# Mamba-2 scan with a gated feed-forward: g in four 32-row products over four PSUM banks, states from 32-column products, two hp banks with a lag of two, running products in halves, another order of the start

**Chip, cores, metric.** One NeuronCore of a Trainium2 chip. Time is device microseconds of one execution. A profile is one execution; its span is mostly 1.7 to 2 us shorter than the time of the same execution.

## The reference, cut to what matters

```python
# attention part: x (4, 8, 768, 32), a (4, 8, 768), B and C (4, 8, 768, 16)
for c in range(nc):                                   # chunks
    L = np.exp(cum[:, :, :, None] - cum[:, :, None, :]) * causal
    y_intra = np.einsum('bhij,bhjd->bhid', (Cc @ Bc^T) * L, xc)
    y_inter = np.einsum('bhin,bhnd->bhid', Cc, state) * np.exp(cum)
    state = decay_full * state + sum_j(Bc x xc * decay_from_j)
# feed-forward part on the rows of y: 3072 tokens, 256 -> 2048 -> 256
h = x @ w_in
g = h * np.cos(h)
out = g @ w_out
```

The kernel works in blocks of 128 steps (six blocks c) with four sequences b of eight heads. The feed-forward part is cut into 96 tiles n of 128 hidden rows by 512 tokens (16 per block). All products are float32. The scan of block c+1 runs beside the feed-forward of block c. "A period" below is three tiles n with one sequence b of the scan among them: its transposes in the first, its `g` in the second, its `y` and states in the third.

## The kernel before

The parts that the change and the argument touch (cuts are marked `# ...`):

```python
BANKS = {"scan": 3, "h": 3, "o": 2}                   # PSUM banks: 8
LAG = 3

def decays(c, b):                                      # running products of a
    # ... c > 0:
    V.tensor_tensor_scan(out=l, data0=arow.pop((c, b)), data1=unit, initial=0.0,
                         op0=ALU.mult, op1=ALU.add)    # 128 x 1024
    V.tensor_tensor_scan(out=r, data0=along[c][:, b], data1=ones, ...)   # reach

def turn(c, b):
    tp = bank([P, 2, P], "tp")
    PE.transpose(tp[:, 0], B...); PE.transpose(tp[:, 1], C...)
    for t in range(HH):                                # 4
        ACT.activation(cT[:, t], tp[:, 1], AF.Copy, scale=slot[:, t:t + 1])
    ACT.copy(out=bcT[:, 0], in_=tp[:, 0])
    V.tensor_tensor(out=bcT[:, 1], in0=tp[:, 1], in1=reach[c, b], op=ALU.mult)

def intra(c, b):
    g = [bank([P, HH, P], "g") for _ in range(2)]
    for u in range(2):
        r = slice(64 * u, 64 * u + 64)
        PE.matmul(g[u], lhsT=bcT[r, 0], rhs=cT[r], start=True, stop=True)
    # ... VectorE: m = g * l

def carry(c, b):
    s_ps = bank([P, H, D], "s_ps")
    PE.matmul(s_ps, lhsT=sc, rhs=xr[:, b], start=True, stop=True)  # 128 x 256
    # ... VectorE: state = s_ps * own + state * reach

for n in range(NC * NF + LAG):
    first(n)       # hp = w_in^T yT; ScalarE: k; VectorE: w
    grade(...)     # ScalarE, GpSimd: conversion of the weights, n < 13
    gate(n - 1)    # ScalarE: Sin; VectorE: gT = hp * cos
    second(n - LAG)   # o += gT^T w_out; at the end of a block, copies of o
    join(...)      # VectorE, GpSimd: conversion of the weights
    # ... carry(0, n); for the next block: decays, then turn, intra or finish
```

## Time and profile before

| | before |
|---|---|
| time, median (range) | 432.41 us (431.49 to 433.74) |
| span of the profile | 430.6 us |
| TensorE busy | 97% |
| hp(0) starts | 27.40 us |
| hp(0) to hp(18), weights converted beside it | 77.2 us |
| a period after that | 13.46 us |

The main lines are in the prediction. For the stages I take the start of the first matmul of hp(n) for each n; a difference between two kernels that changes between hp(i) and hp(j) was won or lost there. The group lines of the two parts that the change aims at, with count, busy time and mean duration in ns:

```profile
L298 PE MATMUL g<-cT,bcT 64*128 64x512 f32 x96 | 27.8, 641 | 0.3 <-ACT bcT L286 0.2
L333 PE MATMUL s_ps<-xr,sc 128*128 128x256 f32 x40 | 13.6, 421 | 0.0
```

Each float32 product shows as two matmul instructions. Their recorded durations contain latency and overlap, so the sums of busy time are no measure of what a product costs the stream; start-to-start distances are.

### The profile page before, as it was taken

How to read it: one execution, taken by the hardware profiler on the slowest of the kernel's cores; microseconds unless marked ns; L12 is line 12 of the kernel's file. 1: busy time of each engine (PE TensorE's matmuls, PEld its weight loads, DVE VectorE, ACT ScalarE, POOL GpSimd, SP SyncE). 2: the span in 40 equal slices, each digit the busy share in tenths (PEclk: the TensorE clock that was granted, in tenths of full speed). 3: DMA queues.
4: the chain of work that ended last, by engine and by line, in shares of the span. 5: the costliest groups of instructions: out<-in, count | busy, mean ns of one | idle time of the engine just before them, and what ended most of it. 6: DMA issues, size and time to landing. Idle time of an engine off the chain costs nothing.

```text
span 430.6 us, 5067 instructions
## 1 busy us (share of the span) xinstructions
PE 419.0 (97%) x1886; PEld 270.4 (63%) x1886; DVE 263.6 (61%) x388; ACT 178.3 (41%) x376; POOL 46.2 (11%) x62
## 2 busy tenths in 40 slices
PE   8988989989999999999999999999999999999996
PEld 8645555656566666666657656566665666666665
DVE  4868998984765574656764467665476555443332
ACT  2457565623443343533433434342343433333332
POOL 2155365340000000000000000000000000000000
PEclk9999999999999999999999999999999999999999
DMA  8999994185301157111129111102010000010001
GB/s 95 329 117 331 318 144 103 34 116 57 98 7 45 49 98 74 52 47 49 50 66 105 50 49 49 50 0 75 0 49 2 0 2 0 2 50 0 0 2 49
DMA packets 105945, 30.25 MB, mean 70 GB/s; under 512 B 75136, under 2 KB 101824, under 8 KB 105920
## 3 DMA queue, kind: packets, MB, share of 16 engines
q1 hardware_dynamic: 105920, 29.92, 34.3%
q8 instruction: 15, 0.25, 0.2%
q14 instruction: 10, 0.08, 0.1%
HBM read 26.57 MB, written 3.34 MB: 69 GB/s over the span
## 4 chain that ended last, share of the span: by engine, by line
PE 81%; DVE 6%; SPq 5%; DMA 2%; ACT 2%; issue 2%; POOL 1%; ACTq 0%; DVEq 0%
PE hp L349 35%; PE o L370 34%; SPq L109 4%; PE g L298 4%; PE y L319 3%; PE s_ps L333 2%; PE y L315 2%; POOL w_in L187 1%; DVE mag L183 1%; DVE lam L250 1%; DMA words<-in_moe_w_out_dram 1%; DVE mag L181 1%; SPq L126 1%; DMA along<-a_all 1%; DVE gT L362 1%
## 5 line engine op out<-in xcount | busy, mean ns | idle before, releaser
L349 PE MATMUL hp<-yT,w_in 128*128 128x512 f32 x384 | 183.3, 600 | 5.2 <-POOL w_in L187 3.2
L370 PEld LDWEIGHTS o<-w_out,gT 128*128 128x128 f32 x768 | 146.0, 190 | 59.4 <-issue 44.5
L370 PE MATMUL o<-w_out,gT 128*128 128x256 f32 x768 | 181.0, 379 | 0.0
L355 DVE SCALAR_TENSOR_TENSOR w<-hp,k 128x512 f32<-128x512 f32 x96 | 66.1, 688 | 120.0 <-ACT k L353 120.0
L353 ACT ACTIVATE k<-hp 128x512 int32<-128x512 f32 x96 | 57.3, 597 | 186.6 <-PE hp L349 186.2
L349 PEld LDWEIGHTS hp<-yT,w_in 128*128 128x128 f32 x384 | 69.3, 190 | 70.7 <-issue 48.2
L360 ACT ACTIVATE w<-w,quarter 128x512 f32<-128x512 f32 x96 | 68.5, 713 | 0.1
L362 DVE TENSOR_TENSOR gT<-hp,w 128x512 f32<-128x512 f32 x96 | 66.1, 688 | 3.9 <-ACT w L360 3.9
L250 DVE TENSOR_TENSOR_SCAN lam<-arow,unit 128x1024 f32<-128x1024 f32 x20 | 46.6, 2330 | 0.0
L284 ACT ACTIVATE cT<-tp,slot 128x128 f32<-128x128 f32 x96 | 27.4, 371 | 20.5 <-PE tp L280 20.5
L301 DVE TENSOR_TENSOR m<-g,lam 128x512 f32<-128x512 f32 x48 | 30.9, 684 | 6.9 <-PE g L298 6.9
L273 POOL TENSOR_TENSOR sc<-bc,lam 128x128 f32<-128x128 f32 x20 | 8.6, 430 | 208.1 <-DVE lam L250 117.4
L298 PE MATMUL g<-cT,bcT 64*128 64x512 f32 x96 | 27.8, 641 | 0.3 <-ACT bcT L286 0.2
L324 ACT COPY yT<-y 128x256 f32<-128x256 f32 x24 | 9.0, 375 | 34.0 <-PE y L319 34.0
L336 DVE TENSOR_TENSOR state<-s_ps,own 128x256 f32<-128x256 f32 x20 | 8.4, 421 | 16.7 <-PE s_ps L333 16.6
L319 PE MATMUL y<-m,xr 128*32 128x128 f32 x384 | 15.9, 279 | 1.1 <-DVE m L301 1.1
L187 POOL TENSOR_TENSOR w_in<-mag,last 128x512 uint32<-128x512 uint32 x8 | 14.0, 1752 | 14.3 <-DVE mag L183 14.3
L187 POOL TENSOR_TENSOR w_out<-mag,last 128x512 uint32<-128x512 uint32 x8 | 12.1, 1511 | 14.5 <-DVE mag L183 11.6
L333 PE MATMUL s_ps<-xr,sc 128*128 128x256 f32 x40 | 13.6, 421 | 0.0
L298 PEld LDWEIGHTS g<-cT,bcT 64*128 64x128 f32 x96 | 7.5, 184 | 8.7 <-ACT w L360 5.6
L315 PEld LDWEIGHTS y<-bcT,state 128*128 128x128 f32 x80 | 12.1, 191 | 1.0
L319 PEld LDWEIGHTS y<-m,xr 128*32 128x32 f32 x384 | 8.9, 109 | 5.9 <-DVE m L301 2.0
(42 smaller groups left out, 177.3 us busy)
## 6 DMA issues: line engine op xcount, KB each, us to landing
arow<-a_cut SPq DMA_DIRECT2D x20, 512.0 KB
words<-in_moe_w_in_dram SPq DMA_DIRECT2D x8, 512.0 KB
words<-in_moe_w_out_dram SPq DMA_DIRECT2D x8, 512.0 KB
out_dram<-ob SPq DMA_DIRECT2D x12, 256.0 KB
xr<-in_x_dram SPq DMA_DIRECT2D x5, 512.0 KB
bc<-in_B_dram SPq DMA_DIRECT2D x5, 256.0 KB
bc<-in_C_dram SPq DMA_DIRECT2D x5, 256.0 KB
along<-a_all SPq DMA_DIRECT2D x20, 64.0 KB
```

The costliest lines, as they stand in the source:

```text
L187: G.tensor_tensor(out=dst.bitcast(U32), in0=bits.rearrange("p (k f) -> p k f", k=k), in1=last.rearrange("p (k f) -> p k f", k=k), op=ALU.add)
L250: V.tensor_tensor_scan(out=l.rearrange("p h i -> p (h i)"), data0=arow.pop((c, b)).rearrange("p h i -> p (h i)"), data1=unit.rearrange("p ...
L284: ACT.activation(cT[:, t], tp[:, 1], AF.Copy, scale=slot[:, t:t + 1])
L298: PE.matmul(g[u], lhsT=bcT[r, 0], rhs=cT[r], start=True, stop=True)
L301: V.tensor_tensor(out=m[:, hs], in0=g[u], in1=l[:, hs], op=ALU.mult)
L319: PE.matmul(y[32 * q:32 * q + 32, t], lhsT=xr[:, b, h], rhs=m[:, h], start=(c == 0 and t == 0), stop=True, tile_position=(0, 32 * q), skip ...
L349: PE.matmul(hp[n], lhsT=w_in[:, k, f * P:(f + 1) * P], rhs=yT[c][:, k], start=(k == 0), stop=(k == KT - 1))
L353: ACT.activation(k, hp[n], AF.Copy, bias=0.25, scale=INV_2PI)
L355: V.scalar_tensor_tensor(out=w, in0=hp[n], scalar=INV_2PI, in1=k, op0=ALU.mult, op1=ALU.subtract)
L360: ACT.activation(cos, cos, AF.Sin, bias=quarter, scale=TWO_PI)
L362: V.tensor_tensor(out=gT[n], in0=hp.pop(n), in1=cos, op=ALU.mult)
L370: PE.matmul(o[c][b // 2][:, b % 2], lhsT=g[:, b * P:(b + 1) * P], rhs=w_out[:, f], start=(f == 0 and b % 2 == 0), stop=(f == NF - 1), skip ...
```

## The change

The intent: TensorE is the bound, so its small products should use the array's parts side by side. `g` contracts over 16 state dimensions per head, so with a mask four heads fit into 64 rows, or two into 32. Four 32-row products run side by side, need half as many columns (256 instead of 512) and write to four banks. With eight banks in all, hp gives up one, and so `gate` moves into its own step. The rest adapts to that.

```diff
-    LAG = 3
+    LAG = 2
-    BANKS = {"scan": 3, "h": 3, "o": 2}
+    def pair(name):                       # two banks at a time, two pairs
+        return psum.tile([P, 2, 4 * P], FP32, tag="scan", bufs=2, name=name)

-        for t in range(HH):
+        for t in range(2):
             ACT.activation(cT[:, t], tp[:, 1], AF.Copy, scale=slot[:, t:t + 1])

-        for u in range(2):
-            r = slice(64 * u, 64 * u + 64)
-            PE.matmul(g[u], lhsT=bcT[r, 0], rhs=cT[r], start=True, stop=True)
+        for u in range(4):
+            r = slice(32 * u, 32 * u + 32)
+            PE.matmul(g[u // 2][:, u % 2, 0:2 * P], lhsT=bcT[r, 0],
+                      rhs=cT[r].rearrange("p t i -> p (t i)"), start=True, stop=True)

-        PE.matmul(s_ps, lhsT=sc, rhs=xr[:, b], start=True, stop=True)
+        for q in range(4):
+            two_ = slice(2 * q, 2 * q + 2)
+            PE.matmul(s_ps[32 * q:32 * q + 32], lhsT=sc[:, two_], rhs=xr[:, b, two_],
+                      start=True, stop=True, tile_position=(0, 32 * q), ...)

 # the loop, step n
             first(n)
+            rest = grade(..., later=True)
+            join(...)
-            gate(n - 1)
+            gate(n)
+            if rest: rest()
         second(n - LAG)
-        join(...)
         # scan of the next block
-                if j == 0: decays(c + 1, b)
+                if j == 0: decays(c + 1, b, 1)     # second half of the scan
                 (turn, intra, finish)[j](c + 1, b)
+            b, j = divmod(f - 2, 3)                # one step sooner:
+            if j == 0: decays(c + 1, b, 0)         # the first half
# cut: the start in another order, with two fills of 512 columns instead of six of 128
# to warm up, y(0, 0) and y(0, 2) in "o" banks and y(0, 1) and y(0, 3) in "h" banks
```

More of the change, by code (lines that the diff above doesn't have):

```diff
@@ L62 @@
     NU = NB * H * NC // RB
-    LAG = 3
+    LAG = 2
+    HP = H // 2
     const = ctx.enter_context(tc.tile_pool(name="const", bufs=1))
@@ L76, with bank @@
     ctx.enter_context(tc.manual_schedule())
-    BANKS = {"scan": 3, "h": 3, "o": 2}
-    def bank(shape, name, tag="scan"):
-        return psum.tile(shape, FP32, tag=tag, bufs=BANKS[tag], name=name)
+    def bank(shape, name, tag):
+        return psum.tile(shape, FP32, tag=tag, bufs=2, name=name)
+    def pair(name):
+        return psum.tile([P, 2, 4 * P], FP32, tag="scan", bufs=2, name=name)
     raw, arow, along = {}, {}, {}
@@ L156, with grade @@
     held = {}
-    def grade(which, i):
+    def grade(which, i, later=False):
         t = words.pop((which, i), None)
@@ L167, in grade, with rest @@
         ACT.activation(mag, high.bitcast(FP32), AF.Abs)
-        last = conv.tile([P, 2 * WC], U32, tag="last", bufs=3, name="last")
-        ACT.activation(last, low, AF.Copy, scale=2.0 ** -29)
         G.tensor_scalar(out=mag, in0=mag, scalar1=MOST, scalar2=LEAST,
                         op0=ALU.min, op1=ALU.max)
+        last = conv.tile([P, 2 * WC], U32, tag="last", bufs=3, name="last")
         held[which, i] = (high, mag.bitcast(U32), last)
+        def rest():
+            ACT.activation(last, low, AF.Copy, scale=2.0 ** -29)
+        if later:
+            return rest
+        rest()
     def join(which, i):
@@ L199 @@
     V.memset(quarter, HALF_PI)
-    unit = const.tile([P, H, P], FP32, name="unit")
-    V.tensor_copy(out=unit, in_=ident.unsqueeze(1).to_broadcast([P, H, P]))
+    unit = const.tile([P, HH, P], FP32, name="unit")
+    V.tensor_copy(out=unit, in_=ident.unsqueeze(1).to_broadcast([P, HH, P]))
     own = const.tile([P, H, D], FP32, name="own")
@@ L209 @@
                     fill=0.0, base=N - 1, channel_multiplier=-1)
-    slot = const.tile([P, HH], FP32, name="slot")
-    V.tensor_tensor(out=slot, in0=own[:, 0:HH, 0], in1=own[:, HH:H, 0], op=ALU.add)
+    slot4 = const.tile([P, HH], FP32, name="slot4")
+    V.tensor_tensor(out=slot4, in0=own[:, 0:HH, 0], in1=own[:, HH:H, 0], op=ALU.add)
+    slot = const.tile([P, 2], FP32, name="slot")
+    V.tensor_tensor(out=slot, in0=slot4[:, 0:2], in1=slot4[:, 2:4], op=ALU.add)
     cut = const.tile([RB, NU, P], FP32, name="cut")
@@ L243, in spread_a, with decays @@
             spread[b].append(a_ps)
-    def decays(c, b):
-        lam[c, b] = l = scan.tile([P, H, P], FP32, tag="lam", bufs=3, name="lam")
-        if c > 0:
-            V.tensor_tensor_scan(
-                out=l.rearrange("p h i -> p (h i)"),
-                data0=arow.pop((c, b)).rearrange("p h i -> p (h i)"),
-                data1=unit.rearrange("p h i -> p (h i)"), initial=0.0,
-                op0=ALU.mult, op1=ALU.add)
+    def decays(c, b, t):
+        if t == 0:
+            lam[c, b] = scan.tile([P, H, P], FP32, tag="lam", bufs=3, name="lam")
+        hs = slice(t * HH, (t + 1) * HH)
+        rows_ = spread[b][t] if c == 0 else arow[c, b][:, hs]
+        V.tensor_tensor_scan(
+            out=lam[c, b][:, hs].rearrange("p h i -> p (h i)"),
+            data0=rows_.rearrange("p h i -> p (h i)"),
+            data1=unit.rearrange("p h i -> p (h i)"), initial=0.0,
+            op0=ALU.mult, op1=ALU.add)
+        if t == 0:
+            return
+        if c > 0:
             reach[c, b] = r = scan.tile([P, P], FP32, tag="reach", bufs=2, name="reach")
@@ L257, in decays @@
                                  op0=ALU.mult, op1=ALU.mult)
-            decay_b(c, b)
-            return
-        for t, a_ps in enumerate(spread.pop(b)):
-            V.tensor_tensor_scan(
-                out=l[:, t * HH:(t + 1) * HH].rearrange("p h i -> p (h i)"),
-                data0=a_ps.rearrange("p h i -> p (h i)"),
-                data1=unit[:, 0:HH].rearrange("p h i -> p (h i)"), initial=0.0,
-                op0=ALU.mult, op1=ALU.add)
-        decay_b(c, b)
-    def decay_b(c, b):
         if c == NC - 1:
@@ L274, in decay_b, with turn @@
                         in1=lam[c, b][:, :, P - 1:P].to_broadcast([P, H, N]), op=ALU.mult)
-    def turn(c, b):
+    def turn(c, b, tag=None):
         bc = raw[c][0]
-        tp = bank([P, 2, P], "tp")
+        tp = (pair("tp")[:, 0] if tag is None else bank([P, 4 * P], "tp", tag)
+              ).rearrange("p (k i) -> p k i", k=4)
         PE.transpose(tp[:, 0], bc[:, 0, heads(b)].rearrange("p h n -> p (h n)"), ident)
         PE.transpose(tp[:, 1], bc[:, 1, heads(b)].rearrange("p h n -> p (h n)"), ident)
-        cT = scan.tile([P, HH, P], FP32, tag="cT", name="cT")
-        for t in range(HH):
+        cT = scan.tile([P, 2, P], FP32, tag="cT", name="cT")
+        for t in range(2):
             ACT.activation(cT[:, t], tp[:, 1], AF.Copy, scale=slot[:, t:t + 1])
@@ L294, in intra, with finish @@
         l = lam.pop((c, b))
-        g = [bank([P, HH, P], "g") for _ in range(2)]
-        for u in range(2):
-            r = slice(64 * u, 64 * u + 64)
-            PE.matmul(g[u], lhsT=bcT[r, 0], rhs=cT[r], start=True, stop=True)
+        g = [pair("g") for _ in range(2)]
+        for u in range(4):
+            r = slice(32 * u, 32 * u + 32)
+            PE.matmul(g[u // 2][:, u % 2, 0:2 * P], lhsT=bcT[r, 0],
+                      rhs=cT[r].rearrange("p t i -> p (t i)"), start=True, stop=True)
         for u in range(2):
             hs = slice(u * HH, (u + 1) * HH)
-            V.tensor_tensor(out=m[:, hs], in0=g[u], in1=l[:, hs], op=ALU.mult)
+            V.tensor_tensor(out=m[:, hs].rearrange("p (k t) i -> p k (t i)", k=2),
+                            in0=g[u][:, :, 0:2 * P],
+                            in1=l[:, hs].rearrange("p (k t) i -> p k (t i)", k=2), op=ALU.mult)
         part[c, b] = (bcT, m)
-    def finish(c, b, fills=0):
+    def finish(c, b, tag=None, fills=0):
         (bcT, m), xr = part.pop((c, b)), raw[c][1]
-        if c > 0:
-            y = bank([P, 2, P], "y")
-        else:
-            y = bank([P, 4, P], "y", "o")
-            fill(y[:, 2:4], fills)
-            y = y[:, 0:2]
+        y = (pair("y")[:, 0] if tag is None else bank([P, 4 * P], "y", tag)
+             ).rearrange("p (k i) -> p k i", k=4)
+        fill(y[:, 2:4], fills)
+        y = y[:, 0:2]
         if c > 0:
@@ L331, in carry @@
         xr, sc = raw[c][1], scaled.pop((c, b))
-        s_ps = bank([P, H, D], "s_ps")
-        PE.matmul(s_ps.rearrange("p h d -> p (h d)"), lhsT=sc.rearrange("p h n -> p (h n)"),
-                  rhs=xr[:, b].rearrange("p h d -> p (h d)"), start=True, stop=True)
+        s_ps = pair("s_ps")[:, 0, 0:2 * D]
+        for q in range(4):
+            two_ = slice(2 * q, 2 * q + 2)
+            PE.matmul(s_ps[32 * q:32 * q + 32], lhsT=sc[:, two_].rearrange("p h n -> p (h n)"),
+                      rhs=xr[:, b, two_].rearrange("p h d -> p (h d)"), start=True, stop=True,
+                      tile_position=(0, 32 * q), skip_group_check=True)
         state[c, b] = new = states.tile([P, H, D], FP32, tag="state", name="state")
-        V.tensor_tensor(out=new, in0=s_ps, in1=own, op=ALU.mult)
+        by_two = "p (k t) d -> p k (t d)"
+        V.tensor_tensor(out=new.rearrange(by_two, k=HP),
+                        in0=s_ps.unsqueeze(1).to_broadcast([P, HP, 2 * D]),
+                        in1=own.rearrange(by_two, k=HP), op=ALU.mult)
         if c > 0:
@@ L346, in first @@
         c, f = divmod(n, NF)
-        hp[n] = psum.tile([P, TB], FP32, tag="h", bufs=3, name="hp")
+        hp[n] = bank([P, TB], "hp", "h")
         for k in range(KT):
@@ L353, in first @@
         ACT.activation(k, hp[n], AF.Copy, bias=0.25, scale=INV_2PI)
-        turns[n] = w = ffn.tile([P, TB], FP32, tag="w", bufs=4, name="w")
+        turns[n] = w = ffn.tile([P, TB], FP32, tag="w", name="w")
         V.scalar_tensor_tensor(out=w, in0=hp[n], scalar=INV_2PI, in1=k,
@@ L366, in second @@
         if f == 0:
-            o[c] = [psum.tile([P, 2, DM], FP32, tag="o", bufs=2, name="o") for _ in range(2)]
+            o[c] = [bank([P, 2, DM], "o", "o") for _ in range(2)]
         g = gT.pop(n)
@@ L382, in second @@
             nc.sync.dma_start(out=rows_[:, 2 * i:2 * i + 2, c, :], in_=ob)
-    tags = (("h", "h"), ("h", "o"), ("h", "h"), ("h", "o"))
-    fill(bank([P, 1, P], "warm", "o"), 6)
-    spread_a(0, tags[0])
-    decays(0, 0)
-    turn(0, 0)
-    spread_a(1, tags[1])
-    decays(0, 1)
+    fill(bank([P, 4, P], "warm", "o"), 2)
+    spread_a(0, ("h", "h"))
+    decays(0, 0, 0)
+    decays(0, 0, 1)
+    spread_a(1, ("o", "o"))
+    turn(0, 0)
+    decays(0, 1, 0)
+    decays(0, 1, 1)
+    intra(0, 0)
+    spread_a(2, ("h", "h"))
+    decays(0, 2, 0)
+    decays(0, 2, 1)
     turn(0, 1)
-    intra(0, 0)
-    spread_a(2, tags[2])
-    decays(0, 2)
+    finish(0, 0, "o")
     intra(0, 1)
-    finish(0, 0)
-    spread_a(3, tags[3])
-    turn(0, 2)
-    decays(0, 3)
-    turn(0, 3)
-    finish(0, 1, 1)
+    grade(*order[0])
+    spread_a(3, ("o", "h"))
+    decays(0, 3, 0)
+    decays(0, 3, 1)
+    turn(0, 2, "h")
+    finish(0, 1, "h", 1)
+    grade(*order[2])
     intra(0, 2)
-    grade(*order[0])
+    turn(0, 3, "h")
     join(*order[0])
     intra(0, 3)
-    finish(0, 2, 2)
     grade(*order[1])
-    grade(*order[2])
-    finish(0, 3, 2)
+    finish(0, 2, "o", 1)
+    finish(0, 3, "h", 2)
     join(*order[2])
@@ L424 @@
         c, f = divmod(n, NF)
+        rest = None
         if n < NC * NF:
@@ L428 @@
             first(n)
-        if c == 0 and n + 3 < len(order):
-            grade(*order[n + 3])
-        if 0 <= n - 1 < NC * NF:
-            gate(n - 1)
+            if n + 3 < len(order):
+                rest = grade(*order[n + 3], later=True)
+            if n + 2 < len(order):
+                join(*order[n + 2])
+            gate(n)
+            if rest:
+                rest()
         if n >= LAG:
             second(n - LAG)
-        if c == 0 and n + 2 < len(order):
-            join(*order[n + 2])
         if n < NB:
@@ L442 @@
                 if j == 0:
-                    decays(c + 1, b)
+                    decays(c + 1, b, 1)
                 (turn, intra, finish)[j](c + 1, b)
+            b, j = divmod(f - 2, 3)
+            if 0 <= b < NB and j == 0:
+                decays(c + 1, b, 0)
             if f == NF - 1:
```

## The prediction

> **What bounds the kernel now.** I read the busy shares first, then the chain that ended last, then TensorE's timeline in an undisturbed stretch, then its waits, and last the start. Busy shares and chain:
>
> ```profile
> PE 419.0 (97%) x1886; PEld 270.4 (63%) x1886; DVE 263.6 (61%) x388; ACT 178.3 (41%) x376; POOL 46.2 (11%) x62
> PE 81%; DVE 6%; SPq 5%; DMA 2%; ACT 2%; issue 2%; POOL 1%; ACTq 0%; DVEq 0%
> ```
>
> TensorE (PE) is never idle after the first tenth, and it is the path. So the kernel shortens by what PE's stream shortens, plus what the start shortens, less any wait that the new order puts into the stream. PE's timeline over one period of the loop (three tiles of the feed-forward part, and one sequence b of the scan beside them) shows what the stream consists of:
>
> ```profile
> 202.53 1.88 PE L349 MATMUL hp<-yT,w_in 128*128 128x512 f32 x4
> 204.25 1.89 PE L370 MATMUL o<-w_out,gT 128*128 128x256 f32 x8
> 205.98 0.27 PE L279 MATMUL tp<-ident,bc 128*128 128x128 f32 x1
> 206.09 0.27 PE L280 MATMUL tp<-ident,bc 128*128 128x128 f32 x1
> 206.19 1.88 PE L349 MATMUL hp<-yT,w_in 128*128 128x512 f32 x4
> 207.91 1.89 PE L370 MATMUL o<-w_out,gT 128*128 128x256 f32 x8
> 209.73 1.13 PE L298 MATMUL g<-cT,bcT 64*128 64x512 f32 x4
> 210.79 1.98 PE L349 MATMUL hp<-yT,w_in 128*128 128x512 f32 x4
> 212.61 1.89 PE L370 MATMUL o<-w_out,gT 128*128 128x256 f32 x8
> 214.34 0.61 PE L315 MATMUL y<-bcT,state 128*128 128x128 f32 x4
> 214.88 0.64 PE L319 MATMUL y<-m,xr 128*32 128x128 f32 x16
> 215.45 0.70 PE L333 MATMUL s_ps<-xr,sc 128*128 128x256 f32 x2
> 215.99 0.59 PE L349 MATMUL hp<-yT,w_in 128*128 128x512 f32 x1
> ```
>
> Durations overlap, so read start to start. A period is 215.99 - 202.53 = 13.46 us. Each hp takes 1.72 (4 instructions, 0.43 per 512 columns), each o 1.73 (0.215 per 256), three of each 10.35. The scan adds the other 3.1: tp 0.21, g 1.06 and two mode changes of 0.1 around it, y 1.1, s_ps 0.54. The change is aimed at g and s_ps.
>
> **What the Trainium skill says.** "TensorEngine Tiling (Array Packing)", Key Properties: tiles of one mode run independently, but changing the mode drains the engine. The trace agrees: before g the start is 0.09 late, and the hp after it takes 1.82 instead of 1.72, as its weight load could not go ahead. "TensorE: Matmul & The Clock Gate", Part 3, gives a measured 3.07 times for four 32-row tiles of 512 columns. This trace shows two row tiles at once: four instructions of 0.43 would be 1.72 in a row, and g lasts 1.06, the two tiles' instructions starting within 0.01 us; no run yet shows four row tiles, but y (L319) shows four column tiles: 16 instructions of 0.107 take 0.57 up to the next group, not 1.7. Part 1 of that page: the clock opens after about 3.4 us of sustained work; here matmuls of 128 columns start every 0.2135 us until 10.25 us and every 0.111 after. "SBUF — State Buffer", Who interferes with whom: a VectorE instruction with two SBUF inputs and a GpSimd instruction that reads SBUF lock each other out, for a whole instruction. The trace agrees (GpSimd's timeline; the first add began just after a 2.28 us scan had):
>
> ```profile
> 56.76 3.17 POOL L187 TENSOR_TENSOR w_in<-mag,last 128x512 uint32<-128x512 uint32 x1 [2.36 <-DVE mag L183]
> 62.95 1.28 POOL L187 TENSOR_TENSOR w_out<-mag,last 128x512 uint32<-128x512 uint32 x1 [1.95 <-DVE mag L183]
> ...
> 59.99 1.98 PE L349 MATMUL hp<-yT,w_in 128*128 128x512 f32 x4 [1.10 <-POOL w_in L187]
> ```
>
> **The change, part by part.**
>
> *g.* Now 0.11 of bare weight load + 2 x 0.427 streaming + 0.10 drain = 1.06. After: eight instructions of 256 columns on four row tiles, so two waves of 0.214: 0.11 + 0.43 + 0.10 = 0.64. Gain 0.427, in 20 of the loop's periods: **8.5 us**. The other four are in the start and counted there.
>
> *States.* Now the last y wave to the end of s_ps is 0.107 + 0.114 drain + 0.107 load + 0.428 = 0.76. After: the four 32-column products stay in y's mode, so no drain before them. Two waves of 64 columns, 0.054 each, then drain and bare load for hp: 0.107 + 0.06 + 0.054 + 0.11 + 0.107 = 0.44. Gain 0.32 in the 16 periods of c = 1 to 4: **5.1 us**. The four at c = 0 save under 0.1 each, as they now need two mode changes.
>
> *Lag of two, two hp banks, gate(n) in step n.* hp(n) waits for gT(n-2). From the end E of an hp the chain is: k, w, Sin, gT. Their spacing in the trace:
>
> ```profile
> 409.64 0.60 ACT L353 ACTIVATE k<-hp 128x512 int32<-128x512 f32 x1 [2.24 <-PE hp L349]
> 410.14 0.71 ACT L360 ACTIVATE w<-w,quarter 128x512 f32<-128x512 f32 x1
> 410.27 0.69 DVE L355 SCALAR_TENSOR_TENSOR w<-hp,k 128x512 f32<-128x512 f32 x1 [2.14 <-ACT k L353]
> ```
>
> E is 409.38, so k ends at E+0.86, w at E+1.58, Sin (0.71) at E+2.32, gT (0.69) at E+3.04. hp(n) starts at E(n-2) + 1.73 + 1.72 + 1.73 = E+5.18: 2.1 us to spare. VectorE's other work per period (two half scans 2.3, reach 0.35, bcT 0.2, m 1.2, two state steps 0.8) goes in after gT; laid out by hand it delays a w by 0.1 to 0.4 at most and never eats the 2.1. So no hp waits in the steady state. One new wait I do find: VectorE's copy of o at the end of a block now stands behind gT, ending at E+3.04+0.6 = E+3.65, and the next o wants its bank at E+3.44: 0.25 us, five times: **-1.2 us**. ScalarE's copy is in time.
>
> *Halved scans.* No less work (2 x 1.14 for 2.28), but GpSimd's adds no longer sit behind 2.28 us. While weights are converted (to about 95 us), three periods took 15.4, 14.6 and 14.5 instead of 13.46: VectorE is 92% busy there and hp waits for GpSimd. After, VectorE has about 13 us of work per period against PE's 12.7, the join now stands in the time gT would wait for Sin, and GpSimd's add starts 0.6 earlier. I count half a us per period over the ideal instead of 1.1 to 1.9: **2 us** more.
>
> *Prologue.* Here it is latency that counts, on three engines. Before, hp(0) starts at 27.40. A hand schedule of the new order with the measured durations (half scan 1.17, cT 0.25 each, g 0.64, eight spread products 1.7 cold or 0.9 warm) gives 27.9 if the clock opens at 10.25 as before, and 26.3 if it opens one window earlier, at about 6.85. The warm-up now streams from 1.28 without a pause into the spread products (before, it ended at 3.85 and PE idled to 4.12), so I expect the earlier window more often: **1 us**. ScalarE's cT halves, but fill and y(0,1) now wait for the last scan's bank. That is why it is so little.
>
> Sum: 8.5 + 5.1 + 2 + 1 - 1.2 = 15.4, and 432.8 - 15.4 = 417.4. I keep 0.6 back for waits overlooked: 418.0.
>
> **Rivals.** (1) *Four row tiles do not run four at once*: they share something the trace's two don't strain, or issue limits them. Then g stays about 1.06, the 8.5 goes and the result is some 427. For it: nothing here has four row tiles. Against: both two row tiles and four column tiles run side by side at full rate, starting 7 ns apart. Chance 7%. (2) *The wait moves to VectorE*: with gate(n) in its own step VectorE stands still for Sin, and with two hp banks any hold-up reaches PE in two steps; g's second pair also waits for bcT (now two banks in rotation, so tp must be read). By my layout bcT ends at E+4.7 and g wants it at E+5.5 in the steady state, but about 0.3 late during conversion. Were VectorE to cost 0.3 us in every period, 6 us go: 424. For it: VectorE's 92% at the conversion. Against: 61% overall, and 2.1 us of room. Chance 12%. (3) *The start gets longer*, or arow and weights come too late by DMA for a scan that is now asked for one step sooner: arow lands near 34.6, and is asked for at about 37. At worst 2 us.
>
> **Range and chances.** The two main gains are counted from spacings seen in the trace and repeat 20 and 16 times; each could miss by a fifth, 3 us together. Conversion and start may be off by 2 each. So 413.5 to 424. A gain of 2% means below 424.2; rival 1, or rival 2 at its full size, would miss it. Faster 0.85, same 0.13, slower 0.02.
>
> **What would show it.** In the changed kernel's profile: a period of 12.7 us; g about 0.64 from its start to the next hp; hp 0.45 after the last y wave; TensorE waiting about 0.25 for the copy of o at five block changes; no hp waiting for gT after 100 us; hp(0) at 26 to 28. The prediction is wrong if g's eight instructions start in four waves instead of two, if the list of TensorE's waits shows gT or bcT in most periods, or if VectorE's idle time before gT (waiting for Sin) comes back as PE idle time.

## The result, and the profile after

| | before | after |
|---|---|---|
| time, median (range), 4 runs each | 432.41 us (431.49 to 433.74) | 415.54 us (414.78 to 416.11) |
| ratio, 95% interval | | 0.9606 (0.9574 to 0.9639) |
| span of the profile | 430.6 us | 414.3 us |
| hp(0) starts | 27.40 | 27.21 |

A ratio is the mean time of one kernel's runs over that of the other's of the same rounds, so it isn't quite the ratio of the medians quoted. The changed kernel is faster by 3.9%, about 16.9 us; predicted were 14.8 us (418.0, from the 432.8 that the prediction set out from). The output is correct, as in every run below.

Busy shares and the chain that ended last, changed kernel:

```profile
PE 404.2 (98%) x2092; PEld 264.2 (64%) x2092; DVE 268.8 (65%) x409; ACT 174.2 (42%) x328; POOL 42.7 (10%) x62
PE 93%; DVE 4%; ACT 1%; issue 1%; DVEq 0%
```

TensorE is still the bound, now with 93% of the chain instead of 81%: most of the waits for others that were left have gone as well. One period in TensorE's timeline (start, duration):

```profile
181.23 1.98 PE L362 MATMUL hp<-yT,w_in 128*128 128x512 f32 x4
...
188.54 0.71 PE L303 MATMUL g<-cT,bcT 32*128 32x256 f32 x8
189.18 1.98 PE L362 MATMUL hp<-yT,w_in 128*128 128x512 f32 x4
...
193.26 0.64 PE L325 MATMUL y<-m,xr 128*32 128x128 f32 x16
193.73 0.29 PE L342 MATMUL s_ps<-xr,sc 128*32 128x64 f32 x8
193.95 1.98 PE L362 MATMUL hp<-yT,w_in 128*128 128x512 f32 x4
```

The period is 193.95 - 181.23 = 12.72 us (13.46 before). g lasts 0.64 to the next hp (1.06 before); from y's first instruction to hp are 0.69 us (1.11 before, from 214.88 to 215.99), but the hp after it now pays 0.1 for its bare weight load, so 0.32 is the net gain. After 95 us the list of TensorE's waits is empty. By stage, from the starts of the hp:

| stage | before | after | won |
|---|---|---|---|
| to hp(0) | 27.40 | 27.21 | 0.2 |
| hp(0) to hp(18) | 77.19 | 73.31 | 3.9 |
| hp(18) to hp(66), 12 periods | 202.78 | 193.96 | 8.8 |
| hp(66) to hp(95), 4 periods, no states | 110.63 | 108.97 | 1.7 |
| hp(95) to the end | 12.63 | 10.85 | 1.8 |

The last line is no gain: with a lag of two, one o less (1.73 us) remains after the last hp, and it was done before hp(18) instead. So the stage hp(0) to hp(18) really won 3.9 + 1.7 = 5.6.

While the weights are converted, g is not at its best. Its second pair waits for VectorE's read of the transposes (`bcT`), and g takes 1.28 instead of 0.64 in the last three of the four periods there (1.55 in the first). In front of that read stands the half scan, which started 0.44 us after an add of GpSimd and takes 1.92 us instead of the 1.21 of the steady state:

```profile
54.86 1.27 POOL L195 TENSOR_TENSOR w_in<-mag,last 128x512 uint32<-128x512 uint32 x1 [0.62 <-DVE mag L191]
55.30 1.92 DVE L262 TENSOR_TENSOR_SCAN lam<-arow,unit 128x512 f32<-128x512 f32 x1
57.33 1.35 PE L303 MATMUL g<-cT,bcT 32*128 32x256 f32 x8
57.63 0.29 DVE L293 TENSOR_TENSOR bcT<-tp,reach 128x128 f32<-128x128 f32 x1
58.61 1.98 PE L362 MATMUL hp<-yT,w_in 128*128 128x512 f32 x4
```

And near the end of the start, TensorE ran at half clock. Its timeline there:

```profile
22.14 1.05 PE L94 MATMUL y<-ones 128*128 128x256 f32 x2
23.11 1.08 PE L325 MATMUL y<-m,xr 128*32 128x128 f32 x16
24.13 1.92 PE L94 MATMUL y<-ones 128*128 128x256 f32 x4
25.98 0.64 PE L325 MATMUL y<-m,xr 128*32 128x128 f32 x16
```

The same 16 instructions of y take 1.08 us at 23.11 and 0.64 at 25.98. The clock record of the trace has full clock from 5.29 to 22.36, half from 22.36 to 25.77 and full from there.

### The profile page after: what moved, and what is told of

It reads as the page before. It is cut to its first block, busy times and chain, and to the rows that moved or that the text cites. A ratio compares the mean times of both kernels' runs of the same rounds, so it can differ in the third digit from the quotient of the medians.

```text
span 414.3 us, 5495 instructions
## 1 busy us (share of the span) xinstructions
PE 404.2 (98%) x2092; PEld 264.2 (64%) x2092; DVE 268.8 (65%) x409; ACT 174.2 (42%) x328; POOL 42.7 (10%) x62
## 4 chain that ended last, share of the span: by engine, by line
PE 93%; DVE 4%; ACT 1%; issue 1%; DVEq 0%
PE hp L362 40%; PE o L383 39%; PE g L303 4%; PE y L325 3%; PE y L321 2%; PE a_ps L251 2%; DVE lam L262 1%; PE warm L94 1%; PE y L94 1%; DVE gT L375 1%; DVE mag L191 1%; PE tp L285 1%; PE tp L284 1%; DVE w L368 0%; ACT cT L289 0%
## 5 line engine op out<-in xcount | busy, mean ns | idle before, releaser
L362 PEld LDWEIGHTS hp<-yT,w_in 128*128 128x128 f32 x384 | 67.8, 190 | 58.2 <-issue 53.7
L262 DVE TENSOR_TENSOR_SCAN lam<-arow,unit 128x512 f32<-128x512 f32 x40 | 51.4, 1285 | 0.0
L303 PE MATMUL g<-cT,bcT 32*128 32x256 f32 x192 | 19.7, 426 | 2.7 <-ACT bcT L291 2.4
L289 ACT ACTIVATE cT<-tp,slot 128x128 f32<-128x128 f32 x48 | 14.6, 353 | 9.7 <-PE tp L285 9.7
L303 PEld LDWEIGHTS g<-cT,bcT 32*128 32x128 f32 x192 | 8.6, 183 | 11.7 <-issue 6.2
L330 ACT COPY yT<-y 128x256 f32<-128x256 f32 x24 | 9.0, 373 | 16.5 <-PE y L325 16.4
L191 DVE SCALAR_TENSOR_TENSOR mag<-words,mag 128x512 uint32<-128x512 uint32 x16 | 14.3, 894 | 0.5
L171 POOL TENSOR_SCALAR mag<-mag 128x512 f32<-128x512 f32 x16 | 12.0, 753 | 17.4 <-ACT mag L170 17.4
L321 PE MATMUL y<-bcT,state 128*128 128x128 f32 x80 | 12.2, 274 | 0.0
L170 ACT ACTIVATE mag<-words 128x512 f32<-128x512 f32 x16 | 10.8, 673 | 1.7 <-DMA words<-in_moe_w_in_dram 1.7
```

Source lines behind the costliest of these rows:

```text
L191: V.scalar_tensor_tensor(out=bits, in0=high, scalar=0xC0000000, in1=bits, op0=ALU.bitwise_and, op1=ALU.bitwise_or)
L262: V.tensor_tensor_scan(out=lam[c, b][:, hs].rearrange("p h i -> p (h i)"), data0=rows_.rearrange("p h i -> p (h i)"), data1=unit.rearrange ...
L303: PE.matmul(g[u // 2][:, u % 2, 0:2 * P], lhsT=bcT[r, 0], rhs=cT[r].rearrange("p t i -> p (t i)"), start=True, stop=True)
L321: PE.matmul(y[:, t], lhsT=s[:, t * P:(t + 1) * P], rhs=bcT[:, 1], start=(t == 0), stop=False, skip_group_check=True)
L362: PE.matmul(hp[n], lhsT=w_in[:, k, f * P:(f + 1) * P], rhs=yT[c][:, k], start=(k == 0), stop=(k == KT - 1))
```

## The experiments

Each is an edit of the changed kernel unless it says otherwise. e1 to e4, e5 to e8 and e9 to e12 were run together, each group on one chip; before was 432.91, 433.11 and 432.96 us in them. e8 turned out to be a twin of the changed kernel (see there) and gives its time once more: 415.38 us, ratio 0.9580. Differences of 1 to 3 us between runs on different chips are read from the ratios as well; 0.001 of a ratio is 0.43 us.

### e1: g undone alone

```diff
-        for u in range(4):
-            r = slice(32 * u, 32 * u + 32)      # into g[u // 2][:, u % 2, 0:256]
+        for u in range(2):
+            r = slice(64 * u, 64 * u + 64)      # into g[u][:, 0], 512 columns
# and four cT copies of one head each again
```

> The changed kernel with g undone alone: two products of 64 rows over 512 columns (one bank each), four cT copies again; states, lag, halved scans and prologue stay. Theory (g's gain is streaming time of row tiles): g takes 1.06 us from its start to the next hp again instead of 0.64, the period grows from 12.72 to 13.15, and the time by 20 x 0.43 = 8.5 us plus up to 1.5 in the prologue: 424 to 425.5. Rival (the four row tiles gained little and the time came from the new order of VectorE and the prologue): under 4 us more, below 419.5.

Measured: 426.21 us (425.67 to 426.75), ratio 0.9842 (0.9825 to 0.9859): 10.7 us slower than the changed kernel. TensorE's timeline of e1:

```profile
220.67 1.13 PE L303 MATMUL g<-cT,bcT 64*128 64x512 f32 x4
221.73 1.98 PE L361 MATMUL hp<-yT,w_in 128*128 128x512 f32 x4
```

1.06 us again, in every period of the steady state, and from hp(0) to hp(95) the loop lost 8.3 us, 20 x 0.42. Another 2.1 us came before hp(0). There the edit brings back the longer g and two more cT copies for each sequence, and the clocks of the two profiles differ too (in e1 it opened at 7.00 and stayed open); how much is due to which isn't settled. So the row tiles' streaming is what g's part wins, and the rival with under 4 us is out.

### e2: the states undone alone

```diff
-        for q in range(4): ...                   # four products of 32 columns
+        PE.matmul(s_ps, lhsT=sc, rhs=xr[:, b], start=True, stop=True)
```

> The changed kernel with the states undone alone: one product of 128 columns over 256. Theory: from the last wave of y to the next hp at full rate 0.76 us instead of 0.44, so 16 x 0.32 = 5 us more: 420.5. Rival (half of the gain is the shorter streaming, but the drain after y only moves behind the states, so little is saved): 2 us more, 417.5.

Measured: 419.58 us (419.02 to 421.24), ratio 0.9695 (0.9666 to 0.9725): 4.0 us slower. Timeline of e2:

```profile
208.51 0.70 PE L340 MATMUL s_ps<-xr,sc 128*128 128x256 f32 x2
209.05 1.88 PE L357 MATMUL hp<-yT,w_in 128*128 128x512 f32 x4
```

0.54 us from s_ps to hp instead of 0.22, and the loop from hp(0) to hp(95) lost 5.1 us, as expected to the tenth. Its start was 1.2 us shorter in the profile, as the clock didn't close there; that difference is of the run, not of the edit.

### e5: the states' part alone, in the kernel before

The same four products put into the kernel before.

> The kernel before with the states' part alone (four 32-column products in place of one of 128). Theory: 16 x 0.32 = 5 us less than before, 427.5, as the drain between y and the states goes; the rest of the profile unchanged. Rival (in the kernel before, VectorE or the bank rotation takes the place): within 2 us of before.

Measured: 428.38 us (426.07 to 429.70), ratio 0.9885 (0.9853 to 0.9918): 4.7 us faster than before by the medians. From hp(18) to hp(63), twelve periods, it won 3.94 us, 0.33 each. The part stands on its own in the steady state. That the whole time came out near the 5 us expected is in part luck: the rest of the profile did not stay unchanged. In its profile hp(0) starts at 25.0 with the clock open from 5.25 us, against 27.4 and 10.26 in the profile of before, though the start is the same code: so the start of the kernel before also varies with the clock. Its clock also closed from 49.6 to 53.0, after a wait of y for m, and hp(0) to hp(18) takes 79.33 instead of 77.19.

### e3: the running products whole again

```diff
-        decays(c + 1, b, 0) one step sooner, decays(c + 1, b, 1) with the transposes
+        one scan of 1024 columns with the transposes (c > 0)
```

> The changed kernel with the running products whole again (1024 columns in one, in the step of the transposes). Theory: VectorE reads the transposes only after the scan, and g's second pair needs that bank: bcT ends near E+5.8 instead of E+4.7 while g comes at E+5.5, so g waits about 0.3 to 0.5 us in each of the 20 periods, more while weights are converted: 7 to 11 us more, 423 to 426, with g waiting for bcT on TensorE's list. Rival (halves matter only against GpSimd during conversion): 1 to 2 us more, and no wait of g after 100 us.

Measured: 426.71 us (426.15 to 427.25), ratio 0.9853 (0.9837 to 0.9870): 11.2 us slower. Timeline of e3, VectorE and TensorE:

```profile
204.12 2.28 DVE L264 TENSOR_TENSOR_SCAN lam<-arow,unit 128x1024 f32<-128x1024 f32 x1
206.32 0.40 DVE L273 TENSOR_TENSOR_SCAN reach<-along,ones 128x128 f32<-128x128 f32 x1
206.82 0.29 DVE L295 TENSOR_TENSOR bcT<-tp,reach 128x128 f32<-128x128 f32 x1
...
206.63 1.24 PE L305 MATMUL g<-cT,bcT 32*128 32x256 f32 x8
207.80 1.98 PE L364 MATMUL hp<-yT,w_in 128*128 128x512 f32 x4
```

g starts at 206.63, but its second pair of banks is the one that held the transposes, and VectorE reads them only at 206.82 to 207.11, behind the scan. g takes 1.17 us, more than with two 64-row products. It does so in all 16 steady periods, and 1.95 to 2.34 during conversion. The rival, that halves matter against GpSimd alone, is out. **The halves aren't a side gain: without them, in this order, the two-pair rotation gives most of g's and the states' gain back.** A whole scan behind the read of the transposes (the order of e11) was not run, so it isn't shown that halves are the only way out.

### e4: the gate one step later, with two hp banks

```diff
-            gate(n)
+        if 0 <= n - 1 < NC * NF:
+            gate(n - 1)
```

> The changed kernel with gate(n-1) instead of gate(n) in step n, as before, but with the two hp banks. Theory (two banks are free only because the gate moved into its own step): hp(n+1) needs gT(n-1), which ends at E(n)+2.2 while hp(n+1) comes at E(n)+1.73: 0.5 us in each plain step (36), 0.3 in each step with a transpose (20), none where g or y stand between: 20 to 26 us more, 436 to 441, and slower than the kernel before. Rival (the order of the gate is indifferent, PE's 2 us of room cover it): within 2 us of 415.5.

Measured: 457.59 us (457.33 to 458.19), ratio 1.0569: 42 us slower than the changed kernel, and slower than before. Timeline of e4 in the last block:

```profile
430.46 1.89 PE L383 MATMUL o<-w_out,gT 128*128 128x256 f32 x8
431.96 0.69 DVE L375 TENSOR_TENSOR gT<-hp,w 128x512 f32<-128x512 f32 x1
432.71 1.98 PE L362 MATMUL hp<-yT,w_in 128*128 128x512 f32 x4 [0.36 <-DVE gT L375]
```

o would be done at 430.46 + 1.73 = 432.19; hp starts at 432.71, behind the gT that frees its bank. A plain step loses 0.62 us (0.5 expected), one with a transpose 0.3. After hp(18) it loses 25 us; the 20 to 26 expected were for the whole loop, so the direction and the cause came true and the size didn't. The other 17 come before hp(18), where the weights' conversion shares VectorE, which my sum had left out; there TensorE also paused once for 3.2 us, and the clock closed from 33.70 to 37.11. So the two hp banks cost nothing only because gate moved into its own step.

### e9: the join behind the second product again

```diff
             first(n)
-            join(...)
             gate(n)
         second(n - LAG)
+        join(...)
```

> The changed kernel with the join of the weights after the second product again, so behind gT instead of ahead of it. Theory: VectorE then stands still for Sin (0.79 us a step) and joins afterwards; with about 13 us of work per period against PE's 12.7 it becomes the bound while weights are converted (n up to 13): 0.8 us more in each of 13 steps, up to 10 us, seen between hp(0) and hp(18) alone; 421 to 426. Rival (the halved scans alone carry the conversion stage): under 2 us more.

Measured: 430.70 us (429.26 to 431.13), ratio 0.9938 (0.9912 to 0.9964): 15 us slower, all of it before hp(18). The direction is as expected, the size beyond it (up to 10). Timeline of e9 around one g:

```profile
60.97 0.70 PE L303 MATMUL g<-cT,bcT 32*128 32x256 f32 x4
63.63 0.83 PE L303 MATMUL g<-cT,bcT 32*128 32x256 f32 x4 [1.97 <-DVE bcT L293]
64.40 3.50 PE L362 MATMUL hp<-yT,w_in 128*128 128x512 f32 x4
```

VectorE stands still for Sin, joins afterwards (about 1 us), then its scan `reach` takes 1.42 us instead of 0.40 beside an add of GpSimd, so it reads the transposes 2 us later; g's second pair waits. The expectation had a loss in each of 13 steps; the runs show it in four periods, at g. In each of four periods the clock then closes for 3.41 us (64.07 to 67.49 here), and the next hp takes 3.3 us instead of 1.7. The wait is paid nearly twice.

### e11: bcT ahead of the second half scan

```diff
 # step of the transposes, VectorE's order
-    second half scan, reach, bcT
+    reach, bcT, second half scan
```

> The changed kernel with reach and bcT (VectorE's read of the transposes) ahead of the second half scan instead of behind it. Theory: g's second pair waits for that read while weights are converted (g takes 1.27 us instead of 0.64 in periods 2 to 4): the wait goes, 0.6 us in each of four periods, 1.5 to 2.5 us less, 413.5, all of it between hp(0) and hp(18). Rival: VectorE's sum of work is the bound there, so the wait only moves to hp or y: under 0.7 us.

Measured: 412.47 us (411.78 to 413.26, 6 runs), ratio 0.9526 (0.9508 to 0.9544): against the twin, 2.3 us less by the ratios and 2.9 by the medians. g takes 0.64 to 0.70 in all periods, and hp(0) to hp(18) takes 71.02 us instead of 73.31: 2.3 us, as expected. GpSimd's add now holds up the short scan `reach` (1.12 us instead of 0.40), the read follows at once, and the half scan behind it takes 1.21 us again. So VectorE's order and not its sum of work was what held g up there.

### e6: fills that keep the clock open

```diff
+        fill(tp[:, 2:4], fills)      # ahead of the transposes
-    turn(0, 2, "h")
+    turn(0, 2, "h", 1)
-    turn(0, 3, "h")
+    turn(0, 3, "h", 2)
```

> The changed kernel with one and two fills of 256 columns in the spare half of the transposes' banks ahead of turn(0,2) and turn(0,3), where TensorE idles 1.4 and 1.3 us. Theory (the clock closed from 22.4 to 25.8 us because of these idle gaps): the clock stays open, y(0,2) and the fills run at full rate, hp(0) starts near 26.0 instead of 27.2: 1.2 us less, 414.3. Rival (the start is bound by ScalarE and VectorE; the clock closes whatever is done, or it costs nothing): within 0.4 us, or slower by the fills.

Measured: 415.19 us (414.47 to 415.57), ratio 0.9585 (0.9570 to 0.9599), against 0.958 for the twin of the same group. In the profile the clock stays open from 5.85 us, and hp(0) starts at 26.46 instead of 27.21. In time, no difference shows. The reason can be seen in the changed kernel's own four runs: two have a mean granted clock of 0.996 and spans of 414.3 and 414.4, two have 0.999 and 413.1 and 413.4. So the closing comes in some runs only and costs about 1.1 us where it comes; the fills cost part of that again (hp(0) at 26.46, against 25.97 and 25.82 in e2 and e3, which have the changed start without fills and whose clock stayed open as well). The time is the rival's, not worth it, though the clock did stay open as the theory had it.

### e7: y(0,1) in an o bank

```diff
-    finish(0, 1, "h", 1)
+    finish(0, 1, "o", 1)
```

> The changed kernel with y(0,1) in a bank of o instead of a bank of h, so that it does not wait for the last half scan of the spread products (TensorE idles 1.42 us there). Theory: what follows (g(0,2), m, the transposes of b=3) moves up by about 1.4 us, hp(0) starts near 25.8, 1 to 1.4 us less. Rival: ScalarE's two weight conversions or the clock[...] set the start, and under 0.5 us is won.

Measured: 413.57 us (413.12 to 413.83), ratio 0.9548 (0.9534 to 0.9562): 1.8 us faster than the twin of the same group by the medians, 1.4 by the ratios. hp(0) starts at 24.89 in the profile, with an open clock. In the changed kernel, TensorE idles 1.42 us ahead of this y, for a bank that the last half scan is still reading; the o bank was free. All four timed runs have a clock of 1.0. That the clock stays open because this idle time is gone isn't shown: e3, whose start still has it, shows 1.0 in its four runs too. And the clock isn't all of the gain: with it open, the start of e2 and e3 reaches hp(0) at 25.97 and 25.82, about 1 us later.

### e10: the start of the kernel before

The operations of the start in their old order, with six short fills and y in o banks; all else as changed.

> The changed kernel with the start of the kernel before (its order of operations, its six short fills, y in the o banks), everything else changed. Theory: the new start wins nothing by itself (hp(0) at 25.8 to 26.0 where the clock stays open, against 25.0 for the old start in the run of the states alone): 0.5 to 1.5 us less where the clocks are alike, 414.5. Rival (the prediction's step: the new start is worth 1 us): 1 us more, 416.5.

Measured: 414.00 us (413.69 to 414.33), ratio 0.9560 (0.9545 to 0.9575): faster than the changed kernel by 1.5 us in the medians, by 2.0 us in the ratios, and than the twin by 0.9 us in the ratios, whose intervals overlap a little. hp(0) starts at 24.37, where the clock opened at 4.00, and hp(0) to hp(18) takes 73.87 instead of 73.31. So the new order of the start wins nothing. Whether it loses isn't settled, as the clocks differ: the changed start with an open clock has hp(0) at 25.97 and 25.82 (e2, e3), but there it opened at 6.01 and 5.71.

### e8: the copies of o swapped

```diff
-            if i:
+            if not i:
                 ACT.copy(out=ob, in_=o[c][i])
```

> The changed kernel with the two copies of o swapped: ScalarE takes the first half, VectorE the second. It tests the failed step of the prediction (0.25 us wait at five block changes). Theory: the pool gives the first tile of the next block the bank of the second half, so now that is the one VectorE empties last, at E+3.65 against E+3.44: a wait of 0.2 us at five block changes for VectorE's copy, 1 us more. Rival (the copy ends early enough in either order): the same time, no wait.

Measured: 415.38 us (413.96 to 416.15), ratio 0.9580 (0.9561 to 0.9599), no wait. But the edit didn't test what it was made for: in the compiled order the first pair of o products of a block waits for ScalarE's copy and the second for VectorE's, in both kernels. The pool didn't rotate strictly; it gave the first tile the bank that ScalarE empties, whichever that was. The changed kernel's timeline shows why there is no wait:

```profile
101.03 0.56 ACT L392 COPY ob<-o 128x512 f32<-128x512 f32 x1
101.77 0.68 DVE L394 COPY ob<-o 128x512 f32<-128x512 f32 x1
102.23 1.89 PE L383 MATMUL o<-w_out,gT 128*128 128x256 f32 x8
```

VectorE's copy ends at 102.45, at E+3.66 as worked out, and o has started at 102.23. That o goes into ScalarE's bank, free since 101.60; VectorE's bank is needed by the fifth instruction, at 103.10.

### e12: both improvements

e7's and e11's edits together.

> Both improvements together: y(0,1) in an o bank and bcT ahead of the second half scan. Theory: the start and the conversion stage are separate, so the gains add: 2.0 us from the first as measured and 1.5 to 2.5 from the second: 411 to 412. Rival: an earlier start only runs into weights that are not there yet (DMA), and the sum is no better than the first alone, 413.5.

Measured: 411.51 us (410.73 to 411.61), ratio 0.9499 (0.9483 to 0.9514). hp(0) starts at 23.66, hp(0) to hp(18) takes 71.30. This is the fastest version: 5.0% faster than before, 4.0 us faster than the changed kernel by medians. By the ratios it is 3.5 us faster than the twin, where the two alone gave 1.4 and 2.3: the gains add, and the start doesn't run into missing weights.

## Why the prediction was right, and which of its steps were not

Against 432.8 - 418.0 = 14.8 us foreseen, the spans of the two profiles differ by 16.3 us. By the prediction's own terms:

| term | predicted | measured |
|---|---|---|
| g | 8.5 | 20 x 0.42 = 8.4 (timeline; 8.3 in e1's loop) |
| states | 5.1 | 16 x 0.32 = 5.1 (timeline; 5.1 in e2's loop) |
| conversion stage, beyond these | 2 | 5.6 - 4 x 0.735 = 2.7 |
| start | 1 | 0.2 |
| copy of o at block changes | -1.2 | 0 |
| held back for waits overlooked | -0.6 | none after 95 us |

- **g and the states** were right in mechanism and size. Four row tiles do run side by side in float32: the eight instructions of g start in two groups of four, each within 0.02 us, 0.32 us apart (188.54 and 188.86 in the changed kernel), and not in four waves. The period came out at 12.72 us against 12.7. e1, e2 and e5 show each alone. Rival 1 (four row tiles don't run four at once) is out: it put the time at some 427 us, and 426.2 is what the kernel takes where the four row tiles are taken away (e1).
- **Lag of two, two hp banks**: "no hp waits in the steady state" was right. e4 shows that this hangs on gate(n) in its own step.
- **The copy of o** is the step that failed: the working assumed that the next block's first o tile takes the bank that VectorE empties. The time of the copy was right to 0.01 us; the bank wasn't. The compiled order with its waits would have told this beforehand: the first pair waits for ScalarE.
- **Halved scans**: the reason given for them failed. GpSimd's adds did fall from a mean of 1.75 and 1.51 us to 1.28 and 1.27, but in e3, with whole scans, they take 1.28 and 1.27 as well, and with halves and a late join (e9) 1.49 and 1.37. Of the two, whichever starts first holds up the other here: before, three of the four adds beside a scan began 0.16 to 0.17 us after it had, and took about 3.2 us (at most 2.1 behind a half scan in e9); in the changed kernel and in e3 they begin ahead of the scan, as the join comes earlier. So the place of the join shortened the adds, and the scan pays for it (1.92 instead of 1.21 us). The halves are also not free: 2 x 1.21 us against 2.28. Their main value is another, and the prediction had it only as a remark under rival 2: the transposes' bank must be read before g's second pair, and whole scans in the same place would have cost 11.2 us (e3).
- **Conversion stage**: bcT was foreseen "about 0.3 late"; g's wait was 0.63, as the half scan ahead of it was held up by GpSimd's add. That it came out near 2 all the same is since the waits of the kernel before went, as foreseen: hp waited 3.2 us in all for GpSimd there, and not at all now. The order of the join carries the stage (e9, 15 us).
- **Start**: the 1 us failed. The schedule of the new order was near (26.3 for a clock that opens at 6.85; e2 and e3 have 25.97 and 25.82 for 6.01 and 5.71). But it was set against an old start whose clock opened at 10.26, and the old start gains from an early clock as well: hp(0) at 25.00 where it opened at 5.25 (e5). So the 1 us came from the clock and not from the order. The earlier opening did come (5.29 against 10.26 us), but the cause given for it, the gap in the old warm-up, isn't shown: the same old warm-up opened at 5.25 in e5 and at 4.00 in e10. What the forecast left out is that the clock could close again, and it didn't weigh the wait of y(0,1) for its bank, which it named, against an order without it (e7, e10).

What stays open: what decides when the clock closes. Pauses of 1.3 to 2 us within a stretch of 3.41 us were followed by a closing here, others of 1.4 weren't (16.5 to 17.9 us in the changed kernel), and e2 and e3 have the same pauses of the start and no closing. And how much of the difference between the starts in e10 and the changed kernel is clock and how much order.

## What to carry to other kernels

Where TensorE is the bound, lay the timeline of one period out from start to start and look for groups that change the tiling mode or leave row or column tiles empty; such gains can be counted to a few hundredths of a us per period, and they came true here. What the smaller number of banks per tile then costs is decided by the order of the readers: who reads the shared bank last, and what stands ahead of that read on its engine. Undoing the parts one at a time shows which of them only pay for each other: here the halved scans and the moved gate and join hold up the other gains (without one of them, 11 to 42 us are lost). What they win by themselves in the kernel before, no run shows.

## What the Trainium skill lacked or had wrong

- "TensorEngine Tiling (Array Packing)", Key Properties, says that a change of mode drains the engine and gives no size. Here a change of mode costs about 0.2 us: some 0.1 of drain and 0.1 of a weight load that could not go ahead. A group of another mode pays it on both sides: g starts 0.10 late behind o, takes 0.64 us for 0.43 of streaming, and makes the next hp 0.10 longer (1.82 for 1.72).
- "TensorE: Matmul & The Clock Gate", Part 1: its table has the clock close after at least one idle window of about 3.4 us. A later section of that part, on a second failure mode, lets short idles close it, but gives no length. Here it closed, for 3.41 us each time, after pauses of 1.3 to 2 us with work around them (22.36 us in the changed kernel; four times in e9), and in other runs not after the same pauses. It opened 4.0 to 10.3 us into the profiles, that is 2.9 to 9.1 us after the first matmul, where the page has about 4; in the kernel before, this was a stream of matmuls with one pause of 0.3 us.
- The same part says that matmuls never start less than about 25 ns apart, and not that this is for one tile; Part 3 of the page has about 4 ns between tiles. Here matmuls on different column tiles start 7 ns apart (the four first of the states at 193.726, 193.732, 193.739 and 193.746 us in the changed kernel's record).
